# Fourth token tile of MLP block 0 turned by VectorE through DRAM, and the order of four deferred query activations, in a two-layer linear attention and MLP kernel

## Chip, cores, metric

One core of one Trainium2 chip. Times are device microseconds of one execution of the program; the time before is 866.67 us, the median of three runs (866.61 to 866.70). Engines: PE (TensorE, matmuls), DVE (VectorE), ACT (ScalarE), POOL (GpSimd), SP (SyncE, which here issues DMAs; ACT issues a few too).

## The reference, cut

x has 2048 tokens of D = 448 values. Two layers, each an attention and an MLP, each behind a layer norm without weights, all in float32:

```
phi(t) = where(t > 0, t + 1, exp(t)) + 1e-6          # on q and k, 16 heads of 28
kv = einsum("bhsd,bhse->bhde", phi(k), v);  z = einsum("bhsd->bhd", phi(k))
o  = einsum("bhqd,bhde->bhqe", phi(q), kv) / (einsum("bhqd,bhd->bhq", phi(q), z) + 1e-6)
x  = x + o.reshape(B, S, D) @ wo
x  = x + gelu(norm(x) @ w1 + b1) @ w2 + b2           # F = 1792, tanh form of gelu
```

## The kernel before, in words

Tokens are worked in 16 tiles of 128, and in MLP blocks of four tiles (512 tokens). For matmuls each operand is split into a rounded part and the rest (XH and XL of the activations, w1h and w1l of a weight), and three of the four products are added up in PSUM.

A layer begins with phase 1: keys of all 16 tiles, their phi, and the sum G of key outer products; queries of tiles 0 to 8 too. Queries 9 to 15 are **deferred**: their matmuls (psq, `stage_q`) are spread over the handover to the MLP, where PE would wait otherwise. At the handover kv is formed and folded into `wo` (Mh, Ml); the four tiles of block 0 are taken through attention (op, `o_mm`), residual and layer norm (`o_ln` L896, `o_n` L914), transposed, split into XH and XL, and the MLP begins. The order is written out by hand as tokens in `ORDER` (L631), and each engine executes its instructions in that order; there is no scheduler. Tokens that matter here:

- `Q`, `Qy`, `Qa`: matmuls of the next deferred query (`Qy` the last eight of query 11's eleven; then 12, 13, 14, 15)
- `Qi` (`phi_first` L576): e = exp(min(q, 0)) on ACT, as e = relu(-q), then e = exp(-e). `Qj` (`phi_last` L583): max(q, 0) + e on DVE, and a DMA of it to DRAM on SP's queue
- `la`, `lb`: residual and statistics of a tile; its norm (xm) on DVE
- `tu` (`turn_xm` L928): DVE transposes a normed tile in 32 by 32 squares into sq, tiles 0 and 1 into one tile (`turn` L298), tile 2 into a half-size one (`turn_one` L320)
- `st` (`store_sq` L307): SP stores sq to DRAM (sq_m). `sp` (`spread` L312): four DMAs read it back in an order that completes the transposition (sp); two are issued by SP and two by ACT, and each waits for the store
- `T` (`m_transpose` L924): four PE transposes of tile 3's norm into a PSUM bank (tp); `o_n` copies 64 columns on ACT for the last of them
- `x` (`m_split` L935): XH is copied by ACT, XL = source - XH by DVE, from sp for tiles 0 to 2 (`split_t` L327) and from tp for tile 3 (`split_x`)
- `pre`: loads of the next block's queries

After ORDER comes the load of the gelu table on ACT (L1150), then `mlp1` (L961) for the first 128 of the 1792 hidden values: eleven matmuls hp, each with 512 columns that are taken from all four tiles, first the seven with XH and then the four with XL. `mlp2` (L981) adds y = gelu(hp) @ w2 with gh and gl, the two parts of the gelu. From there the four blocks run on, PE never without work.

All tiles come from pools that give each tag a few buffers in turn; a new tile waits for the readers of the one that held its buffer. Tags A and B have two buffers each, e three, E two.

Of the kernel before, what the change touches and what calls it, by code (L numbers as in the profile page):

```python
# [22 lines left out]
def linear_attn_mlp_kernel(  # L23
# [49 lines left out]
    def t512(tag, bufs, name, dt=F32, at=0):  # L73
        n = 576 if tag in "BF" else 512
        return work.tile([128, n], dt, name=name, tag=tag, bufs=bufs)[:, at:at + 512]
# [176 lines left out]
    def block(key):  # L252
        if key not in blocks:
            blocks[key] = Block(APART if key[0] == "a" else 0)
        return blocks[key]
# [3 lines left out]
    def transpose_x(xn, tail, key, j, tag="m"):  # L259

        block(key)
        tp = tps[key, j] = bank(tag, 4 if tag == "acc" else 2, "tp")
        for c in range(4):
            pe.transpose(tp[:, c * 128:(c + 1) * 128], xn[:, c * 128:(c + 1) * 128] if c < 3 else tail, ident)
# [8 lines left out]
    def split_x(key, j):  # L273
        tp = tps.pop((key, j))
        hi, lo = blocks[key].pieces(j)
        act.copy(hi, tp)
        dve.tensor_sub(lo, tp, f(hi))
# [17 lines left out]
    def half(name):  # L295
        return work.tile([128, 1024], F32, name=name, tag="S", bufs=5)
# [14 lines left out]

    def spread(key, h, queues=(sp,)):  # L312
        d = stored.pop((key, h))
        r = spreads[key, h] = half("sp") if d.shape[1] == 1024 else t512("A", 2, "sp")
        d = d.rearrange("(i r) (m f) -> m r i f", i=4, m=4)
        for m in range(4):
            eng = queues[m % len(queues)]
            eng.dma_start(r[m * 32:(m + 1) * 32].rearrange("r (i f) -> r i f", i=4), d[m])

    def turn_one(x, key):  # L320
        sq = squares[key, 1] = t512("A", 2, "sq")
        sq = sq.rearrange("p (m c n) -> p c m n", m=4, c=4, n=32)
        dve.transpose(sq[:, :3], x[:, :TL].rearrange("p (c m n) -> p c m n", c=3, n=32))
        dve.transpose(sq[:, 3].rearrange("p (u m) n -> p u m n", u=2),
                      x[:, TL:D].rearrange("p (m n) -> p m n", n=32)[:, None].to_broadcast([128, 2, 2, 32]))

    def split_t(key, t, hi, lo, eng=dve):  # L327

        x = spreads[key, t // 2]
        if x.shape[1] == 512:  # L330
            x = x.rearrange("p (i c n) -> p c i n", i=4, c=4)
        else:
            x = x.rearrange("p (i c u n) -> p u c i n", i=4, c=4, n=32)[:, t % 2]
        h = hi.rearrange("p (c i n) -> p c i n", c=4, n=32)
        act.copy(h, x)  # L335
        eng.tensor_tensor(lo.rearrange("p (c i n) -> p c i n", c=4, n=32), x, f(h), op=OP.subtract)  # L336
# [239 lines left out]
    def phi_first():  # L576
        l, t, o = qo.pop(0)
        e = t512("e" if t < NT - 2 else "E", 3 if t < NT - 2 else 2, "eq")[:, :D]
        act.activation(e, o, AF.Relu, scale=-1.0)
        act.activation(e, e, AF.Exp, scale=-1.0)  # L580
        begun.append((l, t, o, e))

    def phi_last():  # L583
        l, t, o, e = begun.pop(0)
        dve.scalar_tensor_tensor(e, o, 0.0, e, op0=OP.max, op1=OP.add)
        sp.dma_start(pq_d[l][t * 128:(t + 1) * 128, :], e)
# [21 lines left out]
    def stage_g(l, t, acc, mid=lambda: None):  # L608
# [22 lines left out]
    ORDER = [  # L631
# [4 lines left out]
    ] * LAYERS  # L636
    DEFER = NT - sum(tok in ("Q", "Qa", "Qy") for tok in ORDER[0].split())

# [275 lines left out]
    def o_n(l, b, j):  # L914
        t = b * 4 + j
        xn = xns["m", l, t] = ln_norm(sts.pop(("m", l, t)), f"xm{l}_{t}", OP.add if b == 0 else OP.subtract)
        if b == 0 and j == 3:
            act.copy(xn[:, D:], xn[:, TL:D])

    def add_bias(l, b, j):  # L920
        t = b * 4 + j
        pool.tensor_tensor(xt[l, t], xt[l, t], b2b, op=OP.add)

    def m_transpose(l, b, j):  # L924
        xn = xns.pop(("m", l, b * 4 + j))
        transpose_x(xn, xn[:, TL:], ("m", l, b), j)

    def turn_xm(l, j):  # L928
        xn = xns.pop(("m", l, j))
        if j < 2:  # L930
            turn(xn, ("m", l, 0), j)
        else:
            turn_one(xn, ("m", l, 0))

    def m_split(l, b, j):  # L935

        if j < 3:
            split_t(("m", l, b), j, *block(("m", l, b)).pieces(j))
        else:
            split_x(("m", l, b), j)  # L940


    def q_prep(l, b, j, tr):
# [11 lines left out]
    def m_part(l, b, j):  # L955
        split_t(("m", l, b), j, *block(("m", l, b)).pieces(j))
# [159 lines left out]
    for l in range(LAYERS):  # L1116
        tr = SimpleNamespace(mp={})
        za, acc = phase1(l, tr)
        if l == 0:
            background(0)  # L1120
        fill = list(range(DEFER, NT))

        def biases(j):
            if l == 0:
                sp.dma_start(b1s, b1.rearrange("(c p) -> p c", p=128))
                sp.dma_start(b2b, b2[None, :].to_broadcast([128, D]))

        def pre(j):
            for k in range(4):
                load_pq(l, 1, k)  # L1130
            if l == 0:
                background(2)

        tok_ = SimpleNamespace(
            Q=lambda j: stage_q(l, fill.pop(0)), Qp=lambda j: fill_qphi(), Qv=lambda j: stage_qphi(j or 9),
            Qi=lambda j: phi_first(), Qj=lambda j: phi_last(), Qx=lambda j: stage_q(l, fill[0], (0,)),
            Qy=lambda j: stage_q(l, fill.pop(0), (1, 2, 3)),
            Qa=lambda j: stage_q(l, fill.pop(0), tag="acc"), G=lambda j: stage_g(l, NT - 1, acc, lambda: trans_z(tr, zs[l])),
            ld=lambda j: (load_pq(l, 0, j), load_x(l, j)), gt=lambda j: trans_gt(tr, acc),
            kv=lambda j: trans_kv(tr), mask=lambda j: trans_mask(tr), m=lambda j: trans_m(tr, j),  # L1140
            ms=lambda j: trans_ms(tr, j), qz=lambda j: q_z(l, 0, j, tr), qs=lambda j: q_scale(l, 0, j, tr),
            tq=lambda j: q_transpose(l, 0, j), qh=lambda j: q_high(l, 0, j), ql=lambda j: q_low(l, 0, j), o=lambda j: o_mm(l, 0, j, tr),
            la=lambda j: o_ln(l, 0, j), lb=lambda j: o_n(l, 0, j), T=lambda j: m_transpose(l, 0, j),
            x=lambda j: m_split(l, 0, j), tu=lambda j: turn_xm(l, j),
            st=lambda j: store_sq(("m", l, 0), j), sp=lambda j: spread(("m", l, 0), j, (sp, act)), pre=pre, b=biases)
        for tok in ORDER[l].split():
            name, j = tok.rstrip("0123456789"), int("0" + tok.lstrip("abcdefghijklmnopqrstuvwxyzQTG"))
            getattr(tok_, name)(j)
        assert not fill and not qo
        table(AF.Gelu_apprx_tanh)  # L1150
        q_z(l, 1, 0, tr)
        mlp1(l, 0, 0)
        trans_chunks(tr)
        for b in range(NB):
            acc = [bank("acc", 4, f"y{j}")[:, :D] for j in range(4)]
            nxt = b + 1 < NB
            if not nxt and l + 1 < LAYERS:
                st_k = stage_square(wqkv[:, D:2 * D])
                st_q = stage_square(wqkv[:, :D])
                load_to(l + 1, PRE - 1)  # L1160
            for i in range(NF):
                if i + 1 < NF:
                    mlp1(l, b, i + 1)
                elif nxt:
                    mlp1(l, b + 1, 0)
                if l == 0 and b == 0 and i:
                    background(1, 1)
                if i == NF - 2 and not nxt and l + 1 < LAYERS:
                    table(AF.Exp)
                if 9 <= i < 13:  # L1170
                    add_bias(l, b, i - 9)
                if nxt:
                    behind(l, b, i, tr)
                elif l + 1 < LAYERS:
                    if i == 2:
                        split_kq("k", st_k)
                    if i == 5:
                        split_kq("q", st_q)
                    if i in (3, 4, 6, 7, 8):
                        t = (3, 4, 6, 7, 8).index(i)  # L1180
                        stage_a(l + 1, t)
                        stage_n(l + 1, t)
                        stage_t(l + 1, t)
                        if t % 2:
                            stage_sp(l + 1, t)
                    if 9 <= i < 13:
                        stage_x(l + 1, i - 9)
                mlp2(l, b, i, acc)
# [28 lines left out]
```

## Time and profile before

| | |
|---|---|
| median of three runs | 866.67 us (866.61 to 866.70) |
| profiled execution | 866.77 us |
| its span, first to last instruction | 865.0 us |
| PE busy, matmuls | 859.5 us, 4173 |
| DVE, ACT, POOL busy | 489.9, 354.0, 209.1 us |
| granted clock of PE | 1.00 |
| first MLP matmul of layer 0 and of layer 1 (start) | 135.01 and 560.35 us |

Times in rows of the profile are us from the span's start; mean durations are in ns. A row of the timeline gives the start, the duration, engine, line, operation, written tile `<-` read tiles, and how many in sequence were merged (`x3`); in brackets the idle time of the engine before it and what ended that. `SPq` and `ACTq` are transfers being issued, not the transfers. PE's matmuls overlap, so starts tell more than durations. A row of the windows view gives, for one stretch, its length, the busy time of each engine, PE's granted clock, the share of the 16 DMA engines in use, and GB/s. The chain is the work that ended last, followed back from the end.

### The profile page before, as it was taken

What the parts mean: (1) busy time and instruction counts of PE and PEld (TensorE: products, weight loads), DVE (VectorE), ACT (ScalarE), POOL (GpSimd) and SP (SyncE); (2) the same over time, 40 slices, a digit from 0 to 9 for tenths busy, and PEclk for the clock granted to TensorE, in tenths of its full rate; (3) what the DMA queues carried; (4) which work ended last, traced back from release to release, by engine and by line L of the source; (5) the groups of instructions that cost most, each with busy time, mean ns of one, the idle gap of its engine ahead of it and who ended that gap; (6) DMA issues with size and microseconds to landing.
All of it is one profiled execution on the core that took longest, in us unless ns stands there. A gap on an engine that the chain in (4) does not pass through costs nothing.

```text
span 865.0 us, 11671 instructions
## 1 busy us (share of the span) xinstructions
PE 859.5 (99%) x4173; PEld 769.9 (89%) x4173; DVE 489.9 (57%) x956; ACT 354.0 (41%) x634; POOL 209.1 (24%) x242
## 2 busy tenths in 40 slices
PE   9999999999999999999999999999999999999998
PEld 8999988888888888888899998988888888888887
DVE  7888676559455443236477877664674383533112
ACT  6776656333323322333356565632232233223231
POOL 3565612235013012012222343120220140140000
PEclk9999999999999999999999999999999999999999
DMA  5475546633313502051145543362332423111001
GB/s 168 131 241 178 187 112 206 194 112 109 135 60 114 150 0 98 1 182 49 49 149 187 164 129 97 108 217 81 116 107 91 135 74 114 50 49 42 1 1 43
DMA packets 65082, 95.81 MB, mean 111 GB/s; under 512 B 9088, under 2 KB 59904, under 8 KB 65024
## 3 DMA queue, kind: packets, MB, share of 16 engines
q1 hardware_dynamic: 63696, 94.13, 33.8%
q10 hardware_dynamic: 1328, 0.93, 0.4%
q8 instruction: 33, 0.54, 0.3%
q14 instruction: 25, 0.20, 0.1%
HBM read 56.70 MB, written 35.13 MB: 106 GB/s over the span
## 4 chain that ended last, share of the span: by engine, by line
PE 95%; ACT 2%; DMA 1%; DVE 1%; issue 0%; POOL 0%; ACTq 0%; SPq 0%; DVEq 0%
PE hp L972 31%; PE y L1002 10%; PE y L1001 10%; PE y L1003 10%; PE G L622 8%; PE psk L353 8%; PE psq L353 5%; PE op L891 2%; PE op L890 2%; PE op L892 2%; DMA sp<-sq_m 1%; PE op L880 1%; PE op L879 1%; PE op L881 1%; PE kvp L786 1%; PE mp L796 1%
## 5 line engine op out<-in xcount | busy, mean ns | idle before, releaser
L978 DVE TENSOR_TENSOR gl<-g,gh 128x512 fp32r<-128x512 f32 x112 | 83.2, 743 | 293.2 <-ACT gh L977 293.2
L974 ACT ACTIVATE g<-hp,b1s 128x512 f32<-128x512 f32 x112 | 77.1, 688 | 400.1 <-PE hp L972 400.1
L1002 PE MATMUL y<-w2l,gh 128*128 128x448 f32 x447 | 163.6, 366 | 0.0
L1001 PE MATMUL y<-w2h,gh 128*128 128x448 f32 x447 | 162.2, 363 | 0.0
L1003 PE MATMUL y<-w2h,gl 128*128 128x448 f32 x447 | 160.3, 359 | 0.1
L972 PE MATMUL hp<-XH,w1h 128*128 128x512 f32 x336 | 130.7, 389 | 0.0
L972 PE MATMUL hp<-XH,w1l 128*128 128x512 f32 x336 | 130.7, 389 | 0.0
L972 PE MATMUL hp<-XL,w1h 128*128 128x512 f32 x336 | 130.1, 389 | 0.0
L215 POOL TENSOR_TENSOR brs<-bve,mhalf 128x1 f32<-128x1 f32 x55 | 34.8, 632 | 258.4 <-DVE bve L214 257.9
L1001 PEld LDWEIGHTS y<-w2h,gh 128*128 128x128 f32 x447 | 83.7, 187 | 9.8 <-ACT gh L977 0.5
L1002 PEld LDWEIGHTS y<-w2l,gh 128*128 128x128 f32 x447 | 83.9, 188 | 6.9
L1003 PEld LDWEIGHTS y<-w2h,gl 128*128 128x128 f32 x447 | 84.0, 188 | 5.8 <-DVE gl L978 0.9
L972 PEld LDWEIGHTS hp<-XL,w1h 128*128 128x128 f32 x336 | 63.1, 188 | 13.1
L972 PEld LDWEIGHTS hp<-XH,w1h 128*128 128x128 f32 x336 | 63.0, 187 | 10.7
L972 PEld LDWEIGHTS hp<-XH,w1l 128*128 128x128 f32 x336 | 63.1, 188 | 9.9
L977 ACT CAST gh<-g 128x512 fp32r<-128x512 f32 x112 | 69.6, 622 | 3.6
L840 POOL TENSOR_TENSOR pz<-pq,zb 128x448 f32<-128x448 f32 x32 | 37.0, 1162 | 103.3 <-DVE dn L846 67.1
L353 PE MATMUL psk<-wk,XH 128*128 128x448 f32 x210 | 61.8, 364 | 0.0
L353 PE MATMUL psq<-wq,XH 128*128 128x448 f32 x196 | 57.5, 366 | 0.0
L478 POOL TENSOR_TENSOR xnl<-x,xnh 128x384 fp32r<-128x384 f32 x32 | 35.0, 1092 | 69.3 <-ACT xnh L477 56.0
L622 PE MATMUL G<-kh,xnh 128*128 128x448 f32 x128 | 46.8, 368 | 0.0
L336 DVE TENSOR_TENSOR XL<-sp,XH 128x512 fp32r<-128x512 f32 x54 | 45.3, 851 | 2.1 <-ACT XH L335 2.1
(185 smaller groups left out, 1491.1 us busy)
## 6 DMA issues: line engine op xcount, KB each, us to landing
x<-in_A_x_dram SPq DMA_DIRECT2D x32, 224.0 KB, 3.7
pq_d<-eq SPq DMA_DIRECT2D x32, 224.0 KB, 2.7
pq<-pq_d SPq DMA_DIRECT2D x32, 224.0 KB, 3.1
sq_m<-sq SPq DMA_DIRECT2D x14, 512.0 KB, 2.6
x<-x_d SPq DMA_DIRECT2D x32, 224.0 KB, 3.7
sp<-sq_m SPq DMA_DIRECT2D x52, 128.0 KB, 2.8
sq_a<-sq SPq DMA_DIRECT2D x12, 512.0 KB, 2.9
sp<-sq_a SPq DMA_DIRECT2D x48, 128.0 KB, 2.7
```

What stands on the lines that cost most here:

```text
L336: eng.tensor_tensor(lo.rearrange("p (c i n) -> p c i n", c=4, n=32), x, f(h), op=OP.subtract)
L353: pe.matmul(o, x, p, start=(i == 0), stop=(i == 10))
L478: pool.tensor_tensor(lo[:, :TL], xn[:, :TL], f(h[:, :TL]), op=OP.subtract)
L622: pe.matmul(acc[c], w, k, start=first and c not in others[0], stop=last and c not in others[1])
L840: pool.tensor_tensor(pz, pqt[l, b * 4 + j], tr.zb, op=OP.mult)
L972: pe.matmul(o, w, r, start=(k == 0), stop=(k == len(made) - 1))
L974: act.activation(g, hp, AF.Gelu_apprx_tanh, bias=b1s[:, i:i + 1])
L977: act.copy(gh, g)
L978: dve.tensor_sub(gl, g, f(gh))
L1001: pe.matmul(acc[j], gh[:, s], w2h[:, i], start=first, stop=False)
L1002: pe.matmul(acc[j], gh[:, s], w2l[:, i], start=False, stop=False)
L1003: pe.matmul(acc[j], gl[:, s], w2h[:, i], start=False, stop=stop)
```

## The change

Tile 3 of MLP block 0 is no longer transposed on PE. DVE turns it into a half-size square as tile 2 (`turn_one`, now with its own buffers, tag B), and it is stored and spread as tile 2 is; `m_transpose`, `m_split` and the copy in `o_n` go, and `m_part` (L955) splits all four tiles. For queries 12, 13 and 14 the relu on ACT is replaced by min(q, 0) on DVE (`Qm`), and exp follows on ACT (`Qe`). Query 11's `Qi` moves ahead of tile 3's norm. XH and XL of tile 3 are made after query 14's min and exp. The same holds for both layers.

```diff
     def spread(key, h, queues=(sp,)):
...
-        r = spreads[key, h] = half("sp") if d.shape[1] == 1024 else t512("A", 2, "sp")
+        r = spreads[key, h] = half("sp") if d.shape[1] == 1024 else t512("AB"[h - 1], 2, "sp")
...
-    def turn_one(x, key):
-        sq = squares[key, 1] = t512("A", 2, "sq")
+    def turn_one(x, key, h):
+        sq = squares[key, h] = t512("AB"[h - 1], 2, "sq")
...
-        x = spreads[key, t // 2]
+        x = spreads[key, t - 1 if (key, 2) in spreads and t == 3 else t // 2]
...
+    def phi_min():
+        l, t, o = qo.pop(0)
+        e = t512("e" if t < NT - 2 else "E", 3 if t < NT - 2 else 2, "eq")[:, :D]
+        dve.tensor_scalar(e, o, 0.0, None, op0=OP.min)
+        begun.append((l, t, o, e))
+
+    def phi_exp():
+        e = begun[-1][3]
+        act.activation(e, e, AF.Exp)
...
-        "o2 lb0 tu0 la2 o3 lb1 tu1 st0 la3 lb2 tu2 st1 Qy Q lb3 T3 sp0 sp1 Qi Qa x3 Qj x0 x1 x2 Qi Qj pre "
-        "Qa Qi Qj Qa Qi Qj Qi Qj "
+        "o2 lb0 tu0 la2 o3 lb1 tu1 st0 la3 lb2 tu2 st1 Qy Q Qi lb3 tu3 sp0 st2 Qm sp1 Qe Qa sp2 Qj Qj "
+        "Qm Qe Qj x0 x1 x2 pre Qa Qm Qe x3 Qa Qi Qj Qj "
...
-        if b == 0 and j == 3:
-            act.copy(xn[:, D:], xn[:, TL:D])
...
-            turn_one(xn, ("m", l, 0))
+            turn_one(xn, ("m", l, 0), j - 1)
...
-            la=lambda j: o_ln(l, 0, j), lb=lambda j: o_n(l, 0, j), T=lambda j: m_transpose(l, 0, j),
-            x=lambda j: m_split(l, 0, j), tu=lambda j: turn_xm(l, j),
+            la=lambda j: o_ln(l, 0, j), lb=lambda j: o_n(l, 0, j), x=lambda j: m_part(l, 0, j), tu=lambda j: turn_xm(l, j),
```

More of the change, by code (lines that the diff above doesn't have):

```diff
@@ L922, in add_bias @@
         pool.tensor_tensor(xt[l, t], xt[l, t], b2b, op=OP.add)
-    def m_transpose(l, b, j):
-        xn = xns.pop(("m", l, b * 4 + j))
-        transpose_x(xn, xn[:, TL:], ("m", l, b), j)
     def turn_xm(l, j):
@@ L932, in turn_xm @@
         else:
-            turn_one(xn, ("m", l, 0))
[L935 to L940, printed above, removed]
+            turn_one(xn, ("m", l, 0), j - 1)
     def q_prep(l, b, j, tr):
@@ L1135, in linear_attn_mlp_kernel @@
             Q=lambda j: stage_q(l, fill.pop(0)), Qp=lambda j: fill_qphi(), Qv=lambda j: stage_qphi(j or 9),
-            Qi=lambda j: phi_first(), Qj=lambda j: phi_last(), Qx=lambda j: stage_q(l, fill[0], (0,)),
+            Qi=lambda j: phi_first(), Qm=lambda j: phi_min(), Qe=lambda j: phi_exp(), Qj=lambda j: phi_last(), Qx=lambda j: stage_q(l, fill[0], (0,)),
             Qy=lambda j: stage_q(l, fill.pop(0), (1, 2, 3)),
```

## The prediction, made before the run

> **What bounds the kernel now.** The page comes first: TensorE (PE) is busy for 99% of the span, and the chain that ended last is 95% PE work.
>
> ```profile
> span 865.0 us, 11671 instructions
> ...
> PE 859.5 (99%) x4173; PEld 769.9 (89%) x4173; DVE 489.9 (57%) x956; ACT 354.0 (41%) x634; POOL 209.1 (24%) x242
> ...
> PE 95%; ACT 2%; DMA 1%; DVE 1%; issue 0%; POOL 0%; ACTq 0%; SPq 0%; DVEq 0%
> ```
>
> So an edit pays if PE gets less to do, and costs whatever it makes PE wait. The change sits where phase 1 of a layer hands over to the MLP. There, in the chain in order of time for 96 to 146 us, PE is off the chain:
>
> ```profile
> 127.92 3.29 DMA sp<-sq_m
> ...
> 139.98 0.70 DVE gl L978
> ...
> 140.73 0.47 PE y L1003
> ```
>
> The side chain runs through a transfer of tiles 0 to 2, ACT and DVE to the third matmul of the MLP's second product (y). The timeline of PE shows how little of it PE feels:
>
> ```profile
> 125.47 0.37 PE L363 MATMUL psq<-wq,XL 128*128 128x448 f32 x1
> ...
> 127.51 0.36 PE L353 MATMUL psq<-wq,XH 128*128 128x448 f32 x1
> 127.71 0.37 PE L353 MATMUL psq<-wq,XL 128*128 128x448 f32 x1
> 127.92 0.60 PE L264 MATMUL tp<-ident,xm 128*128 128x128 f32 x4
> 128.28 0.45 PE L353 MATMUL psq<-wq,XH 128*128 128x448 f32 x1
> ...
> 135.01 0.39 PE L972 MATMUL hp<-XH,w1h 128*128 128x512 f32 x1
> ...
> 140.00 0.47 PE L1001 MATMUL y<-w2h,gh 128*128 128x448 f32 x1
> 140.31 0.37 PE L1002 MATMUL y<-w2l,gh 128*128 128x448 f32 x1
> 140.73 0.47 PE L1003 MATMUL y<-w2h,gl 128*128 128x448 f32 x1
> ```
>
> Up to 135.01 the deferred queries (psq) hide everything. The only loss is at L1003: with the 0.20 between the two psq rows as the usual step it would start at 140.51, so it waits 0.22 for gl. The first MLP matmul at 135.01 reads all four tiles' XH (mlp1 takes a quarter of each tile per chunk), so it is PE's gate: **whatever is last of the four XH copies sets when PE goes on.** Layer 1 repeats this 425.33 us later:
>
> ```profile
> 566.06 0.47 PE L1003 MATMUL y<-w2h,gl 128*128 128x448 f32 x1
> ```
>
> **What the change removes.** Tile 3's four transposes leave PE. They take 0.36 (127.92 to 128.28), and the psq behind them lasts 0.45 instead of 0.36, 0.08 more: 0.44 us per layer. PE would then reach the MLP at 135.01 - 0.44 = 134.57. ACT loses a copy of 64 columns and three relus, DVE gains three min and two transposes; none of these is an end of the sum by itself, their places are.
>
> **What it adds: a chain for tile 3.** DVE first. Its rows, with the same steps for tile 2 above tile 3's norm:
>
> ```profile
> 124.79 0.51 DVE L227 TENSOR_SCALAR xm<-x,bst,brs 128x448 f32<-128x448 f32 x1
> 125.33 0.58 DVE L323 STREAM_TRANSPOSE sq<-xm 128x384 f32<-128x384 f32 x1
> 125.83 0.27 DVE L324 STREAM_TRANSPOSE sq<-xm 128x128 f32<-128x128 f32 x1
> 126.95 0.51 DVE L227 TENSOR_SCALAR xm<-x,bst,brs 128x448 f32<-128x448 f32 x1 [0.85 <-POOL brs L908]
> ```
>
> The transposes end 126.10 - 124.79 = 1.31 after the norm starts; for tile 3 that is 128.26. Then the store and who waits for it, from the timeline in windows of single transfers (SP and ACT issue halves of each spread):
>
> ```profile
> 125.99 0.29 ACT L906 ACTIVATE bst<-bst,mhalf 128x1 f32<-128x1 f32 x1
> 126.13 0.32 SPq L310 DMA_DIRECT2D sq_m<-sq  x1
> 127.50 0.25 ACT L918 COPY xm<-xm 128x64 f32<-128x64 f32 x1 [1.21 <-DVE xm L227]
> 127.56 0.32 ACTq L318 DMA_DIRECT2D sp<-sq_m  x1
> 128.40 0.30 SPq L318 DMA_DIRECT2D sp<-sq_m  x1
> 128.48 0.37 ACTq L318 DMA_DIRECT2D sp<-sq_m  x1
> 128.88 0.45 ACTq L318 DMA_DIRECT2D sp<-sq_m  x1
> 129.38 0.54 ACT L579 ACTIVATE eq<-psq 128x448 f32<-128x448 f32 x1 [1.64 <-PE tp L264]
> ```
>
> Tile 2's store (256 KB) is issued 0.03 after its transposes, and ACT's first spread that reads it starts 2.35 later (126.13 to 128.48). The L579 row shows what matters: that relu's input, query 11, left PE at 125.47 + 0.37 = 125.84 (L363), yet it starts at 129.38, just after ACT's last issue (128.88 + 0.45). **A transfer issue that waits holds up everything behind it on ACT.** In the new order ACT has: relu and exp of query 11, the spreads of tiles 0 to 2, exp 12, **two spreads of tile 3 that wait for its store**, exp 13, XH of tiles 0, 1, 2, exp 14, XH of tile 3, then query 15. So all four XH copies now stand behind tile 3's store.
>
> Tile 3's store is issued at 128.29. Call A the start of ACT's first spread of tile 3. Alone, as tile 2's was, A = 128.29 + 2.35 = 130.64. But it falls into the spreads of tiles 0 to 2, in which the windows view shows:
>
> ```profile
> 128.00:129.00 1.00, 1.00 (x9) 0.95 (x8) 0.00 (x0) 0.00 (x0) 0.00 (x0) 1.00 0.94 237
> 129.00:130.00 1.00, 1.00 (x7) 0.94 (x6) 0.00 (x0) 0.59 (x2) 0.00 (x0) 1.00 0.88 223
> 130.00:131.00 1.00, 1.00 (x7) 0.92 (x6) 0.00 (x0) 1.00 (x2) 0.00 (x0) 1.00 0.83 222
> ```
>
> (last columns: clock, DMA share, GB/s). Upper end: it moves only after the square of tiles 0 and 1, whose last piece landed at 127.92 + 3.29 = 131.21; ACT now issues its pieces earlier: relu 11 follows L906 at 126.31, exp 11 0.57 later (the step of L579 and L580), and the first issue 0.06 after that (as 127.56 after 127.50), at 126.94 instead of 127.56: 131.21 - 0.62 = 130.6. Then 0.262 MB at 227 GB/s, the mean of the three rows, 1.15, and 0.05 to pick it up: A = 131.8. I take **131.1**, a little under the middle: on SP's queue only half of that square is ahead of the store. [...]
>
> From A to PE, with these rows:
>
> ```profile
> 129.95 0.58 ACT L580 ACTIVATE eq<-eq 128x448 f32<-128x448 f32 x1
> 130.44 0.57 ACT L276 CAST XH<-tp 128x512 fp32r<-128x512 f32 x1
> 131.37 1.66 ACT L335 CAST XH<-sp 128x512 fp32r<-128x512 f32 x3 [0.36 <-DMA sp<-sq_m]
> 137.23 1.28 ACT L204 ACT_TABLE_LOAD   x1
> 131.64 0.61 DVE L585 SCALAR_TENSOR_TENSOR eq<-psq,eq 128x448 f32<-128x448 f32 x1
> 132.18 1.89 DVE L336 TENSOR_TENSOR XL<-sp,XH 128x512 fp32r<-128x512 f32 x3
> ```
>
> Two issues and the start of exp 13: 129.38 - 128.48 = 0.90. DVE gets exp 13 at A + 0.90 + 0.58 + 0.03 = A + 1.51, adds it to query 13 (0.54 to the next), starts XL 0 at A + 2.05, and is through the three XL, less the overlap of two in sequence, about 1.83 later: A + 3.88. ACT's XH 0 to 2 run from A + 0.90 + 0.49 = A + 1.39 to A + 3.05, in time for that. Only now does DVE take min of query 14, as it stands behind XL 2. No row shows this min: it lies between 0.51 (L227, one input, from SBUF) and 0.61 (L585, from PSUM); I take 0.62 with the handover, as it reads PSUM like L585. So A + 4.50; exp 14 on ACT 0.03 later; XH 3 after 0.49; it lasts 0.62 (1.66 less two steps of 0.52); PE 0.04 later: **A + 5.68 = 136.78.** PE had its last psq by 134.57: it idles 2.21.
>
> Covered, and so priced at nothing: tile 3's spread, some 3.2 us after its issue like tile 2's, lands near A + 3.7 and is needed at A + 5.02. SP holds tile 2's spread back behind tile 3's store, from 128.40 to 128.65 and its second piece to about 129.6; with 3.3 to land that is 132.9, and XH 2 wants it at A + 2.43 = 133.5; if the store delays it by 1.15 the chain grows by up to 0.4. XL 3 is not needed until seven matmuls into the first MLP group. Relu 15, exp 15 and the table load (0.52 after XH 3 starts, then 0.57 + 0.58 + 1.28) end at A + 7.97 = 139.07; the first group of the MLP lasts (140.00 - 135.01) / 2 = 2.5, to 139.3, and the second covers gelu, gh and gl. So the 0.22 at L1003 goes away.
>
> **Sum.** Per layer 136.78 - 135.01 - 0.22 = +1.55; two layers +3.10. The profiled execution took 866.77 (span 865.0), so 869.87; the median of the runs shown is 0.10 lower, so **869.8**. Its own range: A = 130.64 and min at 0.51 gives 136.21, +0.98 per layer, 868.6; A = 131.8 gives +2.25 per layer, 871.2.
>
> **Rivals.**
> 1. *The other side: tile 3 is ready when PE is.* Then PE keeps 0.44 per layer, and 0.22 more if the wait at L1003 goes too: 865.8 to 865.35. It decides at A + 5.68 = 135.23 (135.01 + 0.22), that is A = 129.55, 1.26 after the store's issue. For it: PE is bound everywhere else, and 0.44 is sure. Against: tile 2's took 2.35. Chance 0.06.
> 2. *The stall stays, but small.* The store is served at once and lands a little sooner than tile 2's, A = 130.4, with min at 0.51: 135.97, +0.74 per layer, 868.15. For it: store packets may be taken in turn with the spreads' rather than behind them. Against: a DMA share of 0.83 to 0.94. Chance 0.12.
> 3. *The idle 2.2 us costs PE its clock.* How PE runs cold is seen at the start, in its timeline:
>
> ```profile
> 1.12 4.21 PE L170 MATMUL warm<-one 128*128 128x128 f32 x18 [1.12 <-DVE one L164]
> ...
> 5.61 0.61 PE L170 MATMUL warm<-one 128*128 128x128 f32 x4
> 7.07 0.47 PE L567 MATMUL psk<-wk,XH 128*128 128x448 f32 x1 [0.85 <-ACT wk L137]
> ```
>
> The first 18 take 0.23 each, the later four 0.15: at worst some 4.2 us at half speed, 2.1 lost per layer, 874.0. For it: 859.5 of 865.0 us busy leaves no gap of 2.2 to judge by. Against: the matmul after the gap of 0.85 lasts 0.47, as the one at 140.00 does. Chance 0.04. [...]
>
> **Chances and range.** Forecast 0.78, rivals 0.06, 0.12, 0.04. A measurement here tells about 0.2% (1.73 us) from no change: slower begins at 868.40. Forecast and rival 3 are slower: 0.82. Rivals 1 and 2 are within: 0.17, leaving 0.01 for faster than 864.94, which the removed work (0.66 per layer at most) can't reach. Range 868.0 to 871.4: it drops rivals 1 and 3 and part of 2.
>
> **What would show it.** In the changed profile: no L264 row after phase 1; PE idle near 134.6 to 136.8, ended by ACT XH at the first hp; ACT's exp 13 behind a tile 3 spread near 132; DVE's min 14 behind XL 2; L1003 without its 0.22. I am wrong if the store lands under 1.3 us after issue, if PE's first hp starts before 135.2, or if the loss lies outside the two handovers.

## The result, and the profile after

The changed kernel takes 873.93 us (median of six runs, 872.96 to 876.06) where the kernel before, on the same chip, takes 866.78 (866.61 to 867.34): a ratio of 1.0084 (95% interval 1.0073 to 1.0096), 7.15 us more. The prediction was 869.8 with a range of 868.0 to 871.4. The profiled execution took 874.38, 7.61 more than the one of before.

From the page of the changed kernel:

```profile
span 872.7 us, 11685 instructions
...
PE 861.4 (99%) x4165; PEld 771.5 (88%) x4165; DVE 494.1 (57%) x966; ACT 350.9 (40%) x626; POOL 210.0 (24%) x242
...
PE 95%; DMA 2%; DVE 1%; ACT 1%; issue 0%; POOL 0%; SPq 0%; DVEq 0%; ACTq 0%
```

PE has eight matmuls fewer (two layers of four transposes) and is yet busy for 1.9 us longer. That alone says that the loss is not idle time only: some matmuls took longer. The timeline of PE at both handovers (start, duration, engine, line, operation; in brackets the idle time before it and its releaser):

```profile
134.38 0.36 PE L353 MATMUL psq<-wq,XL 128*128 128x448 f32 x1
137.47 0.78 PE L969 MATMUL hp<-XH,w1h 128*128 128x512 f32 x1 [2.73 <-ACT XH L335]
...
144.62 0.36 PE L1000 MATMUL y<-w2h,gl 128*128 128x448 f32 x1
...
566.50 0.50 PE L969 MATMUL hp<-XH,w1h 128*128 128x512 f32 x1 [2.69 <-ACT XH L335]
...
573.63 0.36 PE L1000 MATMUL y<-w2h,gl 128*128 128x448 f32 x1
```

L1000 here is L1003 of the kernel before. Its first y<-w2h,gl stood at 140.73 and 566.06; now it stands at 144.62 and 573.63. So layer 0 costs 3.89 and both layers 7.57 of the 7.61: the loss lies wholly in the two handovers. One part of layer 0's loss is the idle time of 2.73, ended by ACT's XH. The other part shows in the windows view of PE (length, busy time and matmul records, granted clock, DMA share, GB/s):

```profile
134.11:137.52 3.41, 0.68 (x5) 1.00 1.00 324
137.52:140.94 3.42, 3.42 (x8) 0.50 0.98 338
140.94:144.35 3.41, 3.41 (x16) 1.00 0.76 250
564.19:567.60 3.41, 1.09 (x5) 1.00 0.99 312
567.60:571.01 3.41, 3.41 (x10) 0.50 0.46 165
```

Behind each gap PE ran for 3.41 us at **half its clock** (granted 0.50): 8 matmul records in the second stretch, 16 in the third, of the same length at full clock. The two drops last 3.42 and 3.41 and begin 567.60 - 137.52 = 430.08 apart, which is 126 times 3.413. The trace's record of the granted clock has each drop at 3.413, and the full clock for 426.67 between them and for 300.37 from the second to a third half-speed stretch behind the last work (from 871.39): 125 and 88 times 3.4133. So in this trace the clock changed on a grid of 3.413 us, and the work does not keep to it: the two first hp start 566.50 - 137.47 = 429.03 apart. In the first stretch PE had 0.68 of work, in the fourth 1.09.

What held the gate back is in the chain of waits of the changed kernel (start, length, what):

```profile
128.30 3.51 DMA sq_m<-sq
131.84 2.07 DMA sp<-sq_m
133.90 0.53 DVE XL L336
...
135.77 0.55 DVE eq L586
...
136.82 0.61 ACT XH L335
```

and in ACT's timeline:

```profile
131.84 0.85 ACTq L318 DMA_DIRECT2D sp<-sq_m  x2
132.73 0.58 ACT L591 ACTIVATE eq<-eq 128x448 f32<-128x448 f32 x1 [2.86 <-DMA sq_m<-sq]
133.22 1.65 ACT L335 CAST XH<-sp 128x512 fp32r<-128x512 f32 x3
136.34 0.58 ACT L591 ACTIVATE eq<-eq 128x448 f32<-128x448 f32 x1 [1.48 <-DVE eq L586]
136.82 0.60 ACT L335 CAST XH<-sp 128x512 fp32r<-128x512 f32 x1
```

with this row of DVE:

```profile
133.34 0.63 DVE L595 SCALAR_TENSOR_TENSOR eq<-psq,eq 128x448 f32<-128x448 f32 x1 [2.28 <-ACT eq L591]
```

Tile 3's store took 3.51 from issue to landing. ACT waited 2.86 for it with exp 13 and three XH behind, and then 1.48 for DVE's min of query 14 with tile 3's XH behind. That is the predicted chain from the store on. One row of the chain misleads: the 2.07 is a piece of tile 3's spread, and XL 0, the XL of the first tile, does not read it. What XL 0 follows is query 13's addition on DVE (133.34), which waited for exp 13.

### The profile page after: what moved, and what is told of

Same layout as the page of the kernel before. It is cut to its first block, busy times and chain, and to the rows that moved or that the text cites. A ratio compares the mean times of both kernels' runs of the same rounds, so it can differ in the third digit from the quotient of the medians.

```text
span 872.7 us, 11685 instructions
## 1 busy us (share of the span) xinstructions
PE 861.4 (99%) x4165; PEld 771.5 (88%) x4165; DVE 494.1 (57%) x966; ACT 350.9 (40%) x626; POOL 210.0 (24%) x242
## 4 chain that ended last, share of the span: by engine, by line
PE 95%; DMA 2%; DVE 1%; ACT 1%; issue 0%; POOL 0%; SPq 0%; DVEq 0%; ACTq 0%
PE hp L969 32%; PE y L999 10%; PE y L998 10%; PE y L1000 10%; PE G L632 8%; PE psk L353 8%; PE psq L353 5%; PE op L901 2%; PE op L900 2%; PE op L902 2%; DMA sq_m<-sq 1%; PE op L890 1%; PE op L889 1%; PE op L891 1%; PE kvp L796 1%; PE mp L806 1%
## 5 line engine op out<-in xcount | busy, mean ns | idle before, releaser
L1000 PE MATMUL y<-w2h,gl 128*128 128x448 f32 x447 | 160.0, 358 | 0.0
L1000 PEld LDWEIGHTS y<-w2h,gl 128*128 128x128 f32 x447 | 84.0, 188 | 5.0
```

Of the source, the lines that this page charges most:

```text
L1000: pe.matmul(acc[j], gl[:, s], w2h[:, i], start=False, stop=stop)
```

## The experiments

The theory after the result has two parts. **Queue and clock:** tile 3's XH stands on ACT behind issues that wait for tile 3's store and behind a min on DVE that waits for XL 2; the idle time that follows then halves PE's clock. **Rivals:** the transfers alone set the gap, so that no order helps; min on DVE is what costs; the clock falls for a reason other than the idle time. Runs 1 to 4 shared a chip where the kernel before takes 866.19, runs 5 to 8 one with 866.88, runs 9 and 10 one with 866.61; each difference is against the kernel before on the same chip.

**1. The changed kernel with PE's idle time filled**, by 13 matmuls per layer that nobody reads.

```diff
         q_z(l, 1, 0, tr)
+        scrap = bank("m", 2, "scrap")[:, :D]
+        for _ in range(13):
+            pe.matmul(scrap, w1h[:, 0, :128], w1h[:, 0, :D], start=True, stop=True)
         mlp1(l, 0, 0)
```

> The changed kernel with 13 matmuls of 448 columns added between query 15 and the MLP in each layer; nobody reads their result, and they last about 13 x 0.20 = 2.6 us, the length of PE's idle time there. Theory Q+C (tile 3's XH stands on ACT behind tile 3's store, and the idle time that this makes halves PE's clock for 3.4 us): the MLP still starts near 137.5, granted clock 1.00 throughout, so only the 1.65 us of half speed per layer go: 874.0 - 3.3 = 870.6 (870.2 to 871.4). Rival 'the clock falls for another reason than idle time': 873 to 875, drops of the clock still there. Rival 'the added matmuls themselves delay the MLP': over 874.

Measured: 871.56 (871.22 to 871.72), ratio 1.0062 (1.0045 to 1.0079), +5.4. Its PE timeline:

```profile
134.46 2.80 PE L1150 MATMUL scrap<-w1h 128*128 128x448 f32 x13
137.28 0.50 PE L969 MATMUL hp<-XH,w1h 128*128 128x512 f32 x1
...
142.87 0.36 PE L1000 MATMUL y<-w2h,gl 128*128 128x448 f32 x1
...
565.23 0.50 PE L969 MATMUL hp<-XH,w1h 128*128 128x512 f32 x1 [0.53 <-ACT XH L335]
```

The gate is nearly as late (137.28 for 137.47), but y follows 5.59 later instead of 144.62 - 137.47 = 7.15; the granted clock is 1.00 all through. More matmuls, less time: with PE's idle time filled the clock was not lost, and no other reason is needed. The time is above the range that was expected, and by more than the 0.2 that it seems: the range was 3.5 to 4.7 over the kernel before (866.67), and +5.4 was measured. The sum below says why.

**2. The changed kernel with tile 3 split directly behind tile 2** (the order's end; the tokens before it are unchanged).

```diff
-Qm Qe Qj x0 x1 x2 pre Qa Qm Qe x3 Qa Qi Qj Qj
+Qm Qe Qj x0 x1 x2 x3 pre Qa Qm Qe Qa Qi Qj Qj
```

> The changed kernel with one token moved: XH and XL of tile 3 right behind tile 2's, ahead of query 14's min and exp. Theory Q+C: XH 3 then waits for its transfer alone (landed 134.78 in the changed kernel), the MLP starts near 135.5, idle 0.7, no drop of the clock there; but min 14 and exp 14 and the table load come later, so that y waits for the first gelu till about 141.3: +1.3 per layer against before, 869.3 (868.3 to 870.3). Rival 'the transfers set it' (any order is late because tile 3's store and spread take 6.5 us): 872 or more. Rival 'order does not matter, the min on DVE does': 873 to 875.

Measured: 869.18 (869.14 to 869.31), 1.0036 (1.0023 to 1.0049), +3.0; clock 1.00. Rows of PE, then of ACT:

```profile
134.63 0.50 PE L969 MATMUL hp<-XH,w1h 128*128 128x512 f32 x1 [0.47 <-ACT XH L335]
...
140.53 0.47 PE L998 MATMUL y<-w2h,gh 128*128 128x448 f32 x1 [0.62 <-ACT gh L974]
```

```profile
132.40 2.19 ACT L335 CAST XH<-sp 128x512 fp32r<-128x512 f32 x4
136.12 0.58 ACT L591 ACTIVATE eq<-eq 128x448 f32<-128x448 f32 x1 [1.54 <-DVE eq L586]
```

PE's gap shrinks from 2.73 to 0.47, and the four XH run without a break. So at the place where the change puts it, XH 3 waited for its turn on ACT and not for its data: in the changed kernel the last piece of tile 3's spread (issued by ACT at 132.24, 2.5 to landing) was there at 134.8, and XH 3 started at 136.82. The rival of the transfers alone falls. But exp 14, still behind min 14, now makes the table load and gh late, and PE waits 0.62 at y instead.

**3. The kernel before with the min alone**: tile 3 stays on PE; phi of queries 12 to 14 as in the change.

```diff
-lb3 T3 sp0 sp1 Qi Qa x3 Qj x0 x1 x2 Qi Qj pre Qa Qi Qj Qa Qi Qj Qi Qj
+Qi lb3 T3 sp0 Qm sp1 Qe Qa x3 Qj Qj Qm Qe Qj x0 x1 x2 pre Qa Qm Qe Qa Qi Qj Qj
```

> The kernel before with the phi half of the change alone: PE still transposes tile 3, queries 12 to 14 take min on DVE and exp on ACT, query 11's phi is ahead of tile 3's norm. Theory Q+C: no store of tile 3, so nothing on ACT waits long; the MLP starts at 135.0 as before, ACT has three relus less and the 0.22 us wait for gl goes: 866.3 (866.0 to 866.8). Rival 'the min on DVE is what is late': 869 or more.

Measured: 868.30 (868.06 to 868.5), 1.0024 (1.0014 to 1.0033), +2.1. **A miss**: about nothing was expected. PE's gate is where it was (134.84), yet y waits 0.56. Rows of PE, then of ACT:

```profile
140.68 0.47 PE L1011 MATMUL y<-w2h,gh 128*128 128x448 f32 x1 [0.56 <-ACT gh L987]
```

```profile
132.66 0.58 ACT L591 ACTIVATE eq<-eq 128x448 f32<-128x448 f32 x1 [2.35 <-DVE eq L586]
...
136.26 0.58 ACT L591 ACTIVATE eq<-eq 128x448 f32<-128x448 f32 x1 [1.48 <-DVE eq L586]
```

With relu on ACT the exp that follows waits for nobody (129.38 and 129.95 in the kernel before). With min on DVE it waits for whatever stands ahead of the min there: XL 3 and two additions for min 13, XL 2 for min 14. So the min in this order has a price of its own, at y.

**4. The changed kernel without the min**: tile 3 by DVE, relu and exp of queries 12 to 14 on ACT as before.

```diff
-sp0 st2 Qm sp1 Qe Qa sp2 Qj Qj Qm Qe Qj x0 x1 x2 pre Qa Qm Qe x3 Qa Qi Qj Qj
+sp0 st2 sp1 Qi Qa sp2 Qj Qj Qi Qj x0 x1 x2 pre Qa Qi x3 Qa Qi Qj Qj
```

> The changed kernel with the other half alone: tile 3 turned by DVE, queries 12 to 14 with relu and exp on ACT as before, in the same places. Theory Q+C: XH 3 is still behind tile 3's store and three activations more, 137.0; idle 2.3, so 870.4 if the clock stays and up to 873.7 if it drops in both layers. Rival 'the min on DVE is what is late': under 868.5. Rival 'the transfers set it': as the changed kernel, 873 to 875, with the MLP waiting for a transfer.

Measured: 872.31 (871.97 to 872.55), 1.0071 (1.0056 to 1.0086), +6.1. PE's gaps are 2.31 and 2.58, so the min is not what makes them. They also tell something of the clock. Windows of PE, on this execution's grid (stretches of 3.413 us counted from its one drop, at 137.23):

```profile
133.82:137.23 3.41, 1.10 (x6) 1.00 0.87 259
137.23:140.65 3.42, 3.42 (x10) 0.50 0.99 345
560.48:563.89 3.41, 2.64 (x14) 1.00 0.61 209
563.89:567.30 3.41, 1.60 (x7) 1.00 0.91 270
```

The gap of 2.31 lay within one stretch, and the clock fell to 0.50; the longer one of 2.58 was cut in two by the grid, 0.77 and 1.81, and the hp behind it went on in steps of 0.23, as at full clock.

**5. The changed kernel reordered**: both exps ahead of the waits, tile 3's split soon after.

```diff
-Qm sp1 Qe Qa sp2 Qj Qj Qm Qe Qj x0 x1 x2 pre Qa Qm Qe x3 Qa Qi Qj Qj
+Qm sp1 Qe Qa Qj Qj Qm Qe sp2 Qj Qa Qm x0 x1 x2 Qe x3 pre Qa Qi Qj Qj
```

> The changed kernel with its tokens put in the order in which things become ready: min 13 and exp 13 ahead of ACT's wait for tile 3's store, min 14 ahead of the XL of tiles 0 to 2, exp 14 between XH 2 and XH 3, so that XH 3 waits for its transfer alone and the table load is not late. Theory Q+C (the order behind the store is what costs, not the transfer): the MLP starts 0.3 to 0.5 us later than in the kernel before, y does not wait: before + 0.5 us (0 to +1.0). Rival 'the transfers set it': +3 us or more. A gain over before would need tile 3's spread to land some 0.5 us sooner than its 134.8 in the changed kernel.

Measured: 868.35 (867.46 to 870.42), 1.0018 (1.0009 to 1.0027), +1.5. Most of the loss is gone, y waits for nothing, but PE still idles 1.20 and 1.26, and the time is **a miss**: 0 to +1.0 was expected. ACT's rows:

```profile
132.80 0.92 ACTq L318 DMA_DIRECT2D sp<-sq_m  x2
133.89 1.66 ACT L335 CAST XH<-sp 128x512 fp32r<-128x512 f32 x3 [1.58 <-DMA pq_d<-eq]
```

The three XH are still behind ACT's issue for tile 3. The releaser named, a store of query results (pq_d), gave a new suspect: run 9.

**6. The same with tile 2's spread on SP alone**, to leave ACT fewer issues.

```diff
-sp=lambda j: spread(("m", l, 0), j, (sp, act))
+sp=lambda j: spread(("m", l, 0), j, (sp,) if j == 1 else (sp, act))
```

> e5 with the four spreads of tile 2 all issued by SP, behind tile 3's store, instead of two of them by ACT ahead of it. If tile 3's store (3.5 us in the changed kernel, 2.2 for the same size in the kernel before) is slow because other transfers share the engines, it lands 0.2 to 0.5 us sooner and the MLP starts as much sooner: before + 0 us (-0.6 to +0.6). If queues do not matter at all: as e5. If the spread of tile 2 becomes last: +0.5 to +1.5.

Measured: 870.83 (869.42 to 872.16), 1.0045 (1.0032 to 1.0058), +4.0. **A miss**, in the other direction. XH 3 now waits for data, and in layer 1 the clock fell. Rows of ACT, of PE, and PE's windows:

```profile
136.00 0.62 ACT L335 CAST XH<-sp 128x512 fp32r<-128x512 f32 x1 [0.83 <-DMA sp<-sq_m]
```

```profile
563.45 0.50 PE L969 MATMUL hp<-XH,w1h 128*128 128x512 f32 x1 [2.04 <-ACT XH L335]
```

```profile
561.01:564.42 3.41, 1.36 (x6) 1.00 0.93 279
564.42:567.84 3.42, 3.42 (x9) 0.50 0.66 242
```

The store was not served sooner: SP issued it at 128.47 and ACT's first reader started at 132.07, 3.60 later. What goes off ACT's queue goes onto SP's, where tile 3's spread stands.

**7. PE's transposes kept, min on DVE, reordered**: run 3 with min 13 ahead of XL 3 and of the additions, and min 14 ahead of XL 0 to 2.

```diff
-T3 sp0 Qm sp1 Qe Qa x3 Qj Qj Qm Qe Qj x0 x1 x2 pre Qa Qm Qe Qa Qi Qj Qj
+T3 sp0 Qm sp1 Qe Qa Qm x3 Qe Qj Qj Qj Qa Qm x0 x1 x2 Qe pre Qa Qi Qj Qj
```

> The kernel before (PE transposes tile 3) with min and exp for queries 12 to 14 as in e3, but min 13 ahead of XL 3 and min 14 ahead of the XL of tiles 0 to 2, exp 14 behind XH 2. e3 lost 2.1 us although PE's gate stood as before: y waited for the first gelu, as exp 14 and the table load came behind min 14, which stood behind XL 2. Theory 'order in DVE's queue': with min 14 early, the table load ends before the first MLP group and the wait for gl (0.22 per layer) goes: before - 0.4 us (-0.8 to +0.2). Rival 'min on DVE costs by itself': as e3, +1.5 to +2.5.

Measured: **865.82** (865.39 to 866.37), ratio 0.9987 (0.9979 to 0.9996), 1.1 us less than the kernel before, and faster than both kernels of this study. PE's rows:

```profile
140.10 0.36 PE L1011 MATMUL y<-w2h,gh 128*128 128x448 f32 x1
...
140.51 0.36 PE L1013 MATMUL y<-w2h,gl 128*128 128x448 f32 x1
```

No wait at y is left: from the first row to the third (two steps of the usual 0.20) it is 0.41, where the kernel before took 0.73 from 140.00 to 140.73. The 0.22 per layer that L1003 lost are 0.44 of the gain. The rest has no cause shown: the gain is larger than the 0.8 expected at most, but its interval (0.35 to 1.8) reaches down to the 0.44. The min can pay; its place decides.

**8. Run 1 with 6 fillers for 13**, which leaves PE idle for some 1.6 us.

> The changed kernel with 6 added matmuls (1.2 us) instead of e1's 13, so that PE idles 1.5 instead of 2.7 us per layer; the MLP starts at the same time. By the three profiles so far the clock's windows lie on a grid of 3.413 us; it halved where 2.31 us of one window were idle and stayed where 1.81 were. Theory 'idle share of a window': no drop, as e1, 5.4 us over before (4.9 to 6.0). If any idle of over a microsecond halves the clock: 7 to 9 over before.

Measured: 871.61 (871.19 to 874.08), 1.0059 (1.0046 to 1.0073), +4.7, with gaps of 1.61 and 1.69. PE's windows, the first with the whole gap of layer 0 (136.27 to 137.88) in it:

```profile
135.35:138.76 3.41, 1.80 (x9) 1.00 0.99 319
138.76:142.17 3.41, 3.41 (x17) 1.00 0.98 349
```

A stretch of 3.41 with the whole gap in it has 1.80 of work, the least that any stretch there can have; the clock stayed at 1.00. Six fillers bring as much as thirteen; the time is 0.2 under the least that was expected.

**9. Run 5 with the stores of queries 11 and 12 behind tile 3's spread.**

```diff
-Qa Qj Qj Qm Qe sp2 Qj Qa Qm x0 x1 x2 Qe x3 pre Qa Qi Qj Qj
+Qa Qm Qe sp2 Qj Qj Qj Qa Qm x0 x1 x2 Qe x3 pre Qa Qi Qj Qj
```

> The reordered version with the DRAM stores of queries 11 and 12 issued behind tile 3's spread (query 13's min and exp go ahead of all three additions). If those stores are what put the reordered version's XH 0 to 2 later, its PE gap of 1.2 us falls to about 0.9 and the kernel before is missed by +0.8 us (+0.1 to +1.3) in place of +1.5. If the stores do not matter and tile 3's store alone sets it, +1.5 again. No clock drop by either (idle under 1.3).

Measured: 867.2 (866.89 to 869.55), 1.0009 (1.0001 to 1.0018), +0.6. The time is near what was expected of the suspect, but the gaps are not: 1.23 and 1.06, where 0.9 was to be seen. Rows of PE, then of ACT:

```profile
135.58 0.50 PE L969 MATMUL hp<-XH,w1h 128*128 128x512 f32 x1 [1.23 <-ACT XH L335]
...
141.10 0.36 PE L1000 MATMUL y<-w2h,gl 128*128 128x448 f32 x1
```

```profile
131.91 0.85 ACTq L318 DMA_DIRECT2D sp<-sq_m  x2
132.88 1.66 ACT L335 CAST XH<-sp 128x512 fp32r<-128x512 f32 x3 [1.69 <-DMA sp<-sq_m]
```

So the named store was at most a part of it (intervals of runs 5 and 9 overlap), and the releaser misled: in both, XH 0 to 2 start right behind ACT's two issues, and those wait for tile 3's store.

**10. Run 9 with tile 3's spread on SP alone**: no issue on ACT waits for that store.

```diff
-sp=lambda j: spread(("m", l, 0), j, (sp, act))
+sp=lambda j: spread(("m", l, 0), j, (sp,) if j == 2 else (sp, act))
```

> The same with all four pieces of tile 3's spread issued by SP, so that no issue on ACT waits for tile 3's store. If ACT's queue is what holds the four XH copies, ACT takes XH 0 to 2 near 131.5 to 133.1 and XH 3 when the spread has landed, near 134.9: idle about 1.0 us, +0.8 us (+0.2 to +1.6) over the kernel before. If the four issues in sequence on SP and the landing set it, the first hp waits for ACT's XH 3 that itself waits for a DMA, with idle of 1.3 to 1.9, +1.6 to +2.8. No clock drop below 1.8 idle.

Measured: 868.31 (867.58 to 869.56), 1.0019 (1.001 to 1.0028), +1.7. ACT's rows:

```profile
131.50 1.86 ACT L335 CAST XH<-sp 128x512 fp32r<-128x512 f32 x3
...
135.41 0.62 ACT L335 CAST XH<-sp 128x512 fp32r<-128x512 f32 x1 [1.57 <-DMA sp<-sq_m]
```

ACT is through with XH 0 to 2 by 133.36, takes exp 14, and then waits 1.57 for the data, so PE idles 1.33. The second branch of the expectation came: the first hp waits for an XH 3 that itself waits for a DMA. With these two queues the spread either blocks ACT or lands late. Issuing it from a third queue was not tried.

## Why the prediction was wrong, point by point

| per layer, layer 0 | predicted | measured |
|---|---|---|
| PE could go on at | 134.57 | 134.58 (134.38 + 0.20) |
| A, ACT's first spread of tile 3 | 131.1 | 131.84 |
| from A to the first hp | 5.68 | 5.63 (137.47 - 131.84) |
| first hp | 136.78 | 137.47 |
| wait at the first y<-w2h,gl | gone | gone |
| loss by the clock | 0 | 1.63 |
| sum | +1.55 | +3.89 |

The 1.63 is the 7.15 from the first hp to the first y<-w2h,gl less the 5.52 of run 9 (141.10 - 135.58), the same matmuls at full clock. (The difference of the medians is 7.15 too, by chance.) Layer 1's is 573.63 - 566.50 - 5.52 = 1.61.

- **Right, and shown:** what bounds PE (the first hp, which reads all four XH), the 0.44 of the removed transposes, the order of steps from A to the gate, min 14 behind XL 2, XH 3 behind exp 14, and the end of the wait at L1003. Run 2 shows that it is this order that holds XH 3.
- **The step that failed: rival 3, "The idle 2.2 us costs PE its clock", chance 0.04.** It is what happened. The evidence against it was "the matmul after the gap of 0.85 lasts 0.47", and a gap of 0.85 says nothing about one of 2.2; the prediction says itself that the profile had no such gap to judge by. So the loss by the clock stood in the sum at nothing. The clock fell after gaps of 2.73 and 2.69 (changed kernel), 2.31 (run 4) and 2.04 (run 6), with PE at work for 0.68 to 1.36 us of the stretch. The rival's total of 874.0 lies beside the measured 873.93 largely by chance: its 2.1 per layer was 0.47 too dear, the stall was too cheap, and most executions lost the clock in one layer only (see the sum).
- **A term that was too small: A.** I took 131.1 between 130.64 and 131.8, an estimate, as no row of the kernel before shows a store amid spreads; it came at 131.84, at the upper end. This made the gate 0.69 late in layer 0. In layer 1 the gate adds 566.50 - 560.35 - 3.89 = 2.26 where 136.78 - 135.01 = 1.77 was expected, 0.49 more. That the upper bound has the right number is luck, as its steps are not what happened. It had the square of tiles 0 and 1 landed by 130.6 and the store moving only then, for 1.15. But the square's last piece, issued by ACT at 127.20, took 4.3 and landed at 131.5, and the store moved before that. Its 256 KB go as 128 packets of 2 KB, which no other transfer there has. The DMA view counts them as the difference of "under 8 KB" and "under 2 KB"; these are its rows for 128.30 to 129.55 and for 129.55 to 131.25:

```profile
DMA packets 365, 0.34 MB, mean 271 GB/s; under 512 B 34, under 2 KB 365, under 8 KB 365
DMA packets 518, 0.49 MB, mean 290 GB/s; under 512 B 55, under 2 KB 390, under 8 KB 518
```

So the store's packets began 1.25 after its issue and took 1.7 to go out, beside 0.23 MB of spreads. Those of tile 2's store, which had the engines to itself, all lie between 126.9 and 127.7: 0.8 after its issue, in 0.8. The store did not wait for the whole square; it came a little late and then moved at half the pace.
- **The sum:** 3.10 as forecast, 0.69 and 0.49 for the stalls, 1.63 and 1.61 for the clock make 7.52; the profiled execution has 7.57. Without the clock it would have taken 874.38 - 3.24 = 871.14, just within the range, which left the clock out by giving it 4 in 100. That does not hold for the median. One drop takes 0.002 from the mean clock of an execution (half of 3.41 us in 872), and the half-speed stretch after the last work (1.28 us in the profiled execution) takes 0.0007. So the profiled execution's 0.995 is its two drops, and the 0.997 and 0.998 of four of the six executions are one drop each. The two executions in the middle, 873.88 and 873.99, have 0.998. Less one drop of 1.62, the stalls alone come to some 872.3 there, past the range, and run 1, where the clock holds, says about the same: 1.0062 times 866.67 is 872.0, by its interval 870.6 to 873.5. So the clock and the stall were both too cheap, and the stalls cost about 1 us more in the usual execution than in the profiled one. Where that lies is not known, as only one execution has a trace.

What stays open: why the store's packets took twice as long. In 129.55 to 131.25 the 16 DMA engines were busy throughout (a share of 1.02 at 290 GB/s, 0.32 MB on one queue and 0.17 on the other), so sharing them with the spreads is what I take as the reason, but no run shows it. Run 6 shows that fewer transfers on ACT's queue, with more on SP's, do not shorten the store (3.60 to the reader).

## What to carry to other kernels

Price an idle stretch of the busiest engine twice: once as idle time, and once as the clock that it may cost afterwards (here 1.6 us a drop); before the second is struck out, the profile must hold gaps of that size behind which the clock held. One is not enough, as the 2.58 of run 4 shows. When work goes from one engine to another, or a transfer is issued from a compute engine, read what stands behind the wait: here tile 3's data was there at 134.8 and its XH started at 136.82, and the same edits cost between 0.6 us (run 9) and 7.2 us by their order alone. And a removed 0.44 us of PE work is a small prize to put a DRAM round trip of 6.5 us (128.30 to 134.8) on its path.

## What the runs showed of the hardware

In the stretches read from the traces of these runs the granted clock fell to 0.50 for 3.41 us (less where the execution ended), and only where PE had little work in the 3.41 before:

| idle time of the gap in its stretch | work in the stretch | clock in the next |
|---|---|---|
| 2.73 (changed kernel, layer 0) | 0.68 | 0.50 |
| 2.34 (changed kernel, end of the last work, 867.98 to 871.39) | 1.07 | 0.50, to the end |
| 2.31 (changed kernel, layer 1: of its 2.69, what lies behind 564.19) | 1.09 | 0.50 |
| 2.31 (run 4, layer 0) | 1.10 | 0.50 |
| 2.04 (run 6, layer 1) | 1.36 | 0.50 |
| 1.81 (run 4, layer 1) | 1.60 | full, by hp steps of 0.23 |
| 1.61 (run 8, layer 0, in 135.35 to 138.76) | 1.80 | 1.00 |

So in these executions the clock fell with 1.36 us of work or less in 3.41 and held with 1.60 or more; nothing between was measured. One drop cost about half its length, 1.63 and 1.61 us in the changed kernel. The stretches stood differently against the work each time: the drop began 0.05 and 1.10 us after the first hp in the changed kernel, 0.43 in run 4 and 0.97 in run 6, and run 4's 2.58 cost no drop where its 2.31 did. That is how I read that the changed kernel's six executions show a mean clock of 0.995 (two drops) or of 0.997 and 0.998 (one), and times within 3.10 us, where those of the kernel before lie within 0.73. What holds in other executions stays open: one of run 8 took 874.08 at a mean clock of 0.998 and one of run 5 took 870.42 at 0.997, which by the same count is a drop each, without a trace to show their gaps.
